# A Fourier mixer and a squared-ReLU feed-forward on one core: the end of the first batch under the order table, squares on GpSimd, two more tiles by seven products

## Chip, cores and metric

The kernel runs on one core of one Trainium2 chip. The metric is the device time of one execution in microseconds (us). Before the change it is 809.88 us, the median of three runs (809.78 to 810.07). The core has five engines that matter here: TensorE (PE, with its weight loads PEld), VectorE (DVE), ScalarE (ACT), GpSimd (POOL) and SyncE (SP, which issues DMAs). PE writes PSUM banks; ACT and DVE read them; GpSimd works on SBUF alone.

## What is computed

```python
X = np.fft.rfft(x, axis=1)                       # x: 8 batches x 3008 x 256
Yr = Xr @ w_r - Xi @ w_i + b_r
Yi = Xr @ w_i + Xi @ w_r + b_i                   # both soft-thresholded at 0.01
y = np.fft.irfft(Y, n=3008, axis=1)
...
h = y.reshape(24064, 256) @ w_in                 # 256 -> 2048
r = np.maximum(h, 0.0)
out = (s * (r * r) + b) @ w_out                  # 2048 -> 256, float32
```

## The kernel before

**The two transforms.** 3008 is taken as 94 x 32, so each transform is a DFT over 94, one over 32, and back, all as matrix products in float16. Batches 1 to 7 go through four stages (`s1_units`, `s23_units`, `s4_units`) whose results pass through DRAM (tiles u/us and v/vs); they are cut into small units and laid between the products of the feed-forward. Batch 0 has nothing to hide behind, so `first_batch` (L550) runs it by itself: twelve steps of `mix` (L602), `fwd_dft` (L630: products into a PSUM bank, a ReLU into m on ACT, a combination into z on DVE) and `inv_dft` (L656: products, then a copy into vt), then `turn` (L674: a transposition by a product with the identity, and a copy into vs) and `last_dft` (L690: products with C_t, and a copy into yt). yt holds y; the feed-forward reads it.

**The feed-forward** goes by 47 tiles of 512 rows (`_tile_order`, L139; tiles 0 to 3 are the "wide" ones of batch 0). For each tile `first_mm` (L1125) makes h in pairs of PSUM banks (psh): two 128x512 products for each of 16 blocks of 128 hidden columns. For each pair of blocks a ReLU takes the two banks to an SBUF tile rt (three of them in turn; L1154 on ACT or L1156 on DVE), and a square takes rt to gt (L1163 on ACT or L1165 on DVE). The second product of tile i is laid between the first products of tile i+1. It has two forms. `second_mms` (L1241) uses 64 products of 128x256. `seven_mms` (L1340) splits the 512 rows and the 256 output columns in halves and uses seven half-size products instead of eight, 112 products of 128x128; for that DVE makes eight sums and differences of parts of gt for each tile (`s_op`, L1306, L1325; the fourth kind may be a DMA with addition instead, issued from POOL, L1317), T_s holds the combined weights, and seven additions (L1390) take the results out, where the direct form needs two (L1278). `seven(ti)` (L1473) chooses: tiles 3 to 45 by seven, tiles 0, 1, 2 and 46 directly.

**What sets the order.** Up to the end of `first_batch` a framework schedules each engine's instructions, and the first of ACT and DVE to be free by a running cost sum takes a copy (`evac`, L233; `act_first`). Behind it `pe["on"]` is set (L1490) and the order is written out by hand: PE's order is the order of the Python code, and each other piece of work is recorded by `later` (L266) and emitted where the table `TURNS` says, which gives for each piece its delay in the sequence and its engine. `need` only asserts that a piece has been emitted. Waits come from data and from buffers: a PSUM bank is written again only when its readers are done.

**Banks.** While batch 0 runs, four single banks form the pool psm (`mix_bank`), two psf (`one_bank`), two psa (`other_bank`). When `first_batch` returns, psm is closed, and its space becomes two pairs of banks, psh (`two_banks`), for the first products.

**The end of batch 0.** All of `first_batch` but `rest` (the last turns and last_dfts) is ahead of the hand-written part. The units of stage 1 of batch 1 (`more`: one 94-row product of 512 columns and a copy into u each) are used there as filler by `some` (L717); the 9 slots from slot 0 on take the others.

Of the kernel before, what the change touches and what calls it, by code (L numbers as in the profile page):

```python
# [26 lines left out]
    "1t1t221o251l1p1y1k251o1s251h1q2i2q362q181p18181t151820181p1c203o1l201g1l294f7b1b3b1b3j15151h"  # L27
    "101p1x0w11150w201h0w14182w192h3h5m564v7j590l0p0x111m12221i000h042c7h0d0l0p0t1u121a1y040o1o08"
    "0p0d0t19213e262e2q050p0w2c0l1519212a2y3a2e080s280c0l2t3y4a090p0t1h2a2y2i1m081029090l0t1h2529"
    "3m4e2q2e0w1g002i040o191c3811191h1x3i2u1y420o0w181p4y260h0t0x1d1h1x262u361y04360s180p0x2p141s"  # L30
    "11151d1h3e2q2a2u0g111l0w1g111h1t292e3e2e2q0t360s182p363e0l0x19191h413p2x31080w1t0c0p151t2d2d"
    "352t35081e080q0c350k0w1k2k101y111a1c1k1l2k2d2i32141e2i2u3i4i0w160t0s1p153i101o0x1x141g1i151g"
    "1l1k1s1h3m4y191i1t2p111s1t10181v15203s141m1x0x102l1p191p2t14181c1m1d2q101c341f63191l1c1s1h3e"
    "175n1d1d1h181l212l3u0x1h1q2y0s0s1w0p260s450s1d0t0y161l210w2w0x1w2h0z0w2k1h0t0w1h3t1d0w1w1d1l"
    "1s1l1p201t1j5z1c1l1l1l1k1o1h1x1l321g1p1g2c1h1h1p212i36222i0s1s0p0u0s2d2l1g310p340x1517141s1x"
    "19101h1v1t1x252935423m4a320g1p0x0w101c101p15141k150z5r1l15181w1d21181l192y1k2k1h1h1p2d3e2i3q"
    "2q0s3q0o110p0y0k1l2d0w1k0t0w3t0z151s2d1p0x0w1v1l1c1s201g1x1l3q191l1t1x2h3m3a4m2e0s180w161828"
    "0x11141518201529151p196q1t1y19181s1c1h1s241h1q1h21212h19212l3d463y4m3a10240d0c4a0n0o0y0o2d11"
    "0l0o13150p0s1k0w0x101k2k191h1p2149354d3125312d250c2y0g100h0p0y0p102g1t3d0h1p4i2a1u0c0u0g2k0w"
    "1d2i1g25151e1m11212h0w1g2c1d1g1q3a3u3l2d2m0s2g190l1d11101l101114282e3y191i1420111h1l1x1l2p1g"  # L40
    "1p1y1c1g1h1u1k24191u2d2h1d1o3k1d1h1j1k1o2k1t1h1g1r1h1p1g2k1h1l1m1p1x2h1j5v1c1l1k201h3y1f5z1c"
    "1p1d1c1o1t251615192q1d141w151a181l15161t29182w191c291b182w1l1114211j1h101t1d1o291p1o241l1n6z"
    "1k1t1l1t1k1t1l2h1t1y1c1l181o1h1x25293m2q2y260w1g0t0y0w1x29102h14240p0x39102g1p0x101h1n1p1h1p"
    "29313q363q3y0c1k0x0w1019181x15141g150z6z1l19181o1p1x151l213a1g1k1d1l1x1x2a363e3m0w3q0w180l1y"
    "0s1l2d14380h0l150r11142s1l0x141r1h141h2s1c251d421h1h1p2d2h3y3i2u2e0o0x0w3m101s0x0l0w1h0w1k21"
    "2d0l3t0x2m1l260t0w1k141h1s241d1q1h1l2h2x1h1x293h463m464e10240h0g460r0s120s30190x0o17190t0w1l"
    "101114182k191h1p212x4d2h2x3p1t1t2d0g6e0k1s0h0s2i0h0s2g1l3p0l111u164e0o420s290p191i141w111a1i"
    "1m1u0p1p290k142o1d141i3a3a3h2d2i0k2c150d1d110k1t1d0x0w202q3u1x26142011191c25191l1w1h2y1c1s1g"
    "1q1p24151q2d2p181d381l1c1r1c1w2x1t19181v1l1c1l2g1g1p1i1o1o2h2j6f1d1h1g2o1d1e1f631g1l1c1g2k1d"
    "1p2215191i1h14211d1i1k1s191i1t1x1g3015292917182x19111o21130t0w1p191o2c1o21281h1j771c2d1h1l1o"  # L50
    "2k1d1h1t1y181l182c1h1l252d2m3m2m2u0w1k0t0y0p1p2h0t2l0w281d0p1n0w2k1t0x0w1p1r1p1p1x2l35424a3i"
    "320c1l0t1010180x311h101c110v5b191g0w1h112d181p1x22101g19293p414e4m5e4u0w1m0w180l0u0l191l142w"
    "0l0k0x0r0x0w30190p0w1f1p0s0w290x1d1g6q151d1t2d3h4u3y423e0w150w4u0w1c0s0t0w11141c0t1x0t290p2u"
    "113u0h0g100k11181k151q111x1x2l0x212x3d4i423e3q0g20050s460f0s3q0s2w0x0l0k0z150t0s1h0w0x10141s"
    "191h1x254l2x3l292p3d3p2p0h1q0o100l0o0y0p142c39410l0x221m4m0y1y4m081y08250h112i101w0x1a1i1m0s"
    "1t2d0s1c281d1c1m3q3u3125560s20150d1b11141h1l1118202a3y101a101w111d1h1o1h1t1h1p2q181l1c1m1c1o"
    "1h222d2p1d1g351l1d1r1c1k2w1t1d1g1z1l1c1g2s1k1p1i1p1o1w1n6b1h1l1x2k1h3i1f4z1c1h181c2819292m11"
    "151e140x201016181p191m1p251c301d2d2x1f101c1d0t1s2131150w1s191p281k1k241h1j771d1p1t1l1o2g1l1t"
    "1h321c1l1c2g1d1h1p2d2u323i2a0s190p0u0s1p2h0w2h0w1w1d0p1j0w381t0x1g1p1r1t1l1x2d353q3y4a320c0s"
    "0t10111d143d1h101c110v571910182g1519181l192q14281d1h4d4l4u5i525i0t120o110l1210191t142s0l0k0x"  # L60
    "0r0t0s2o150t0s170x0o0w2h0x1h142i0t191d252p3q463q4q0o1k0w4q0s1g150t111h141c2d2l0t290x1215260l"
    "0o140t1g1k1w1h221h1x252l1925313h3q4a3y4e142c0l0k1m0r0s120s34110p0w171h11101p1419181g201h1p1x"
    "252x3l3t2x311x3h1t0p4q0o100l0o3q0p0w2c1t3h0l0p320k0y0k250w191i181w0x1a11212p101k2w1l1k1y3a3u"
    "1j2c2m102g190l1d150w211g1115282e2i1c1m1824151h1l291p2p1k1l2u1g1k1l1u1k20191m292d1d1o301d1h4t"
    "1g1k291p1d1c1r1h181o2d1l1p1i1k1l1s2b5z181l1c1s1h46175f1d1p19181t1h212q101h1q0w101s101i141h11"
    "1i1p25182s1d1s2t1f102p1d0t1l1x2d150s1w191g1w1p24281p1j6z1h2l1h1t1k2g191p1d42181l182l1d1h1l1t"
    "263a2i220s180t160o252l102h102w150t1f0w2s1p15141l1n1t1h1p292h3a3q2i36081o11111024111d1p102s15"
    "17571d1w1c1x191d1g1p1x261k2l191l1x4l4q52565a0o1m0s1g0p0u0s1h1t141w0p0o3t0v0t0s1o190t0x1f110s"
    "181s0x2118720t111x2d2p2u4a3a2q0h1c0s4q0s1w0p0t0w0x0w1k2d310p2l0x1i0x1i0x0w1c0x1d1c1w1d1i1g1t"
    "212l191h3d3p3y424a4i1020110g0q170s3y0w1c150p0p171d0t18200s151d1024191h1p214l294125292x2l2l0c"  # L70
    "220w1w0h0s1a0h0s28313p0p1h4y1i4y0t5y0o2g0p111a0w1p1122321e1i1y0q0c1h250c102k19101e323e35292i"
    "0g250x09190t0c1s100t10281y2i1t221824151h1l211p2p1k1t2i1g1k1l1u1k21191y292h1c1k381h1g1n1k1o3d"
    "1t1h1g1v1l1c1l211g1l1m1o1o2c1l1o1s2g1h3a1h1p1h1k2g2h2t2215191e1c1128142a1g1x1d1i212d1k301h20"
    "2l1f1c2o1p151c251n1d141x1h1s201o1p241p1o211l1p1s251p391l1u1g1t1k1s1l1p1x2d3m2u322a101k0x1210"
    "1h29142l18241d111n14381t1h1o1x1x1h1t292h313i323y3m0k0w0x0x0w1c111l151424111t141c2t111p1d1x1p"
    "1u1c1s1l252d455m4q5246105y0w1g0t0y0w1d1h101s0p142d0r110s20110p13150p0s290w1p15151h2d314e3y36"
    "3e0g0w191i0s100p141h181o0x25141h1136191c1o1h1p1w1p1y1c1l212h1h212t354a3u363e0o100t13143m101k"
    "110t0w13151d141g191h1k1w1h1l1t213x2x253d3l251t1t0s1s0p0s2y0p0o1w152t193y1a3e1e0k240l191m1820"
    "151i1m1q212h1k0x2s151s1y3236290w281h0t1j190w1s1d1h2036361c1t1d1h1k241h1p1d1m181l1s241p1u2d2h"
    "1d1o381d1h1j1k1o2d1p1h1k1v1h1g1o2c1p1p1p1o1x1l1s1s291p1p1p1o1s1w1x2d1h1p2q1p1g211h39411c1o19"  # L80
    "1e1t211g20151f1c2g1l19291l1c1g1h1h211o2d1l1t1k1s1l1x1x2u1g1t1k1o1p1u1x251k28151n1o2d1t1h2p1l"
    "1k1w1h1k1p1o2l1l1p1o1w1l1l1p1u1s1s1t1w1p1y21251o28191n1o291t1h2p1l1k1x1l1k1o1o2c1l1p1o241l1l"
    "41421h1l1k1o1h1m1t1x1g2d151f1g1o1h192p1d1g1w1d1c1p1o1w1l1t1w291l1p1p2u2e1u1m1u141h1k1s1l1y21"
    "211o2k19391k1s1l1d2d1h1h1t1h1g1k1o281l1p1o1x1l1x3l3q1g1l1k1o1h1m1t1x1g24151f1g2d1h192d1d1g1w"
    "1h1k2c1o1s1l1p1p1t1x1y1k241o211l1m1t1u1x221l1q1t1u"
# [64 lines left out]
def kernel(  # L150
# [115 lines left out]
    def later(emit, cost, needs=(), frees=None):  # L266

        op = SimpleNamespace(emit=emit, cost=cost, needs=list(needs), gone=False)
        if frees is not None:
            reads[id(frees)].append(op)  # L270
        if pe["on"]:
            pieces.append(op)
            return op
        e = min(cost)
        if "act" in cost:
            e = "act" if act_first(cost["act"], cost["dve"]) else "dve"
            work(e, cost[e])
        begin(op, e)
        return op
# [270 lines left out]
    def first_batch():  # L550
# [49 lines left out]
        zt = {}  # L600

# [28 lines left out]
        def fwd_dft(ec, u):  # L630
            ps = one_bank().rearrange("p (j e) -> p j e", j=4)
            g = gs.pop((ec, u))
            for j in range(4):
# [12 lines left out]
            pos = mpool.tile([P, 4, P], F32, name="m", tag="m")  # L646
            nc.scalar.activation(out=pos, in_=ps, func=AF.Relu, bias=neg_lam)
            z = gpool.tile([P, 4, P], F16, name="z", tag="gt")
            nc.vector.scalar_tensor_tensor(
                out=z, in0=ps, scalar=LAM, in1=pos, op0=ALU.add, op1=ALU.min  # L650
            )
            work("act", 0.69)
            work("dve", 0.69)
            zt[(ec, u)] = z

        def inv_dft(ec, u):  # L656
            ps = other_bank()
            z = zt.pop((ec, u))
            for j in range(4):
                matmul(  # L660
# [925 lines left out]
```

## Time and profile before

| | us |
|---|---|
| median of three runs | 809.88 |
| the profiled execution, its own time | 810.04 |
| its span (first to last instruction) | 808.2 |
| PE busy in the span | 799.2 |
| DVE busy | 758.9 |
| ACT busy | 749.4 |
| POOL busy | 107.0 |
| first product of the feed-forward starts | 44.85 |
| last matrix product starts | 804.08 |

The profiled execution took 810.04 us, 1.84 us more than its span, and stands 0.16 us above the median. A timeline row gives start, duration, engine, line, what is written and read, and how many instructions were merged. A matrix product's duration has its latency in it (0.22 us for 128 columns); products follow each other faster than that, so what one costs PE is read from the start of one to the start of the next. Likewise ACT and DVE start the next instruction some 0.08 to 0.11 us before the row of the last one ends.

### The profile page before, as it was taken

To read this page: it belongs to the slowest core of one execution; us is meant where nothing else is said; L and a number is where in the kernel's file an instruction comes from. 1 tells how busy PE (TensorE), PEld (TensorE's weight loads), DVE (VectorE), ACT (ScalarE), POOL (GpSimd) and SP (SyncE) were. 2 spreads that over 40 slices of the span, in tenths; PEclk is the share of its full clock that TensorE was granted. 3 is DMA by queue.
4 is the path that set the end of the run, shared out by engine and by line. 5 is a ranking of instruction groups with operands and counts; after the bars stand their busy time and mean duration, and the time that the engine had idled before them with its cause. 6 is when DMAs were issued, how large, how long until landed. Compare 5 with 4: busy or idle time off the path is not lost.

```text
span 808.2 us, 22126 instructions
## 1 busy us (share of the span) xinstructions
PE 799.2 (99%) x9006; PEld 613.1 (76%) x9006; DVE 758.9 (94%) x1342; ACT 749.4 (93%) x932; POOL 107.0 (13%) x151
## 2 busy tenths in 40 slices
PE   8999999999999999999999999999999999999998
PEld 7857767777777977788777886778867788777876
DVE  5899999999999999999999999999999999999895
ACT  5989999999999999999999999999999999998984
POOL 4540001110110101111011210012000100000000
PEclk9999999999999999999999999999999999999999
DMA  8983387555774658665686666666556434732213
GB/s 205 190 194 78 95 237 184 102 136 153 208 151 86 153 139 226 145 124 113 169 200 145 135 145 161 152 154 136 137 164 177 108 80 119 183 67 58 62 41 79
DMA packets 120766, 112.89 MB, mean 140 GB/s; under 512 B 9933, under 2 KB 98129, under 8 KB 120665
## 3 DMA queue, kind: packets, MB, share of 16 engines
q1 hardware_dynamic: 102409, 80.55, 36.0%
q0 software_dynamic: 18256, 30.94, 23.2%
q8 instruction: 70, 1.15, 0.6%
q14 instruction: 31, 0.25, 0.1%
HBM read 53.52 MB, written 46.66 MB: 124 GB/s over the span
## 4 chain that ended last, share of the span: by engine, by line
PE 93%; DMA 0%; ACT 0%; DVE 0%; issue 0%; DVEq 0%; ACTq 0%
PE psh L225 40%; PE psa L225 34%; PE psf L225 19%; DMA out_dram<-ost 0%; DVE ost L1278 0%; ACT rt L1154 0%; ACT u L288 0%; DVEq L1278 0%; ACTq L1154 0%
## 5 line engine op out<-in xcount | busy, mean ns | idle before, releaser
L225 PE MATMUL psh<-yt,w_in 128*128 128x512 f16 (+3 forms) x1792 | 444.5, 343 | 0.2 <-ACT rt L1154 0.2
L225 PEld LDWEIGHTS <-gt 128*128 128x128 f16 x4400 | 306.7, 98 | 141.7 <-DVE gt L1325 2.4
L1154 ACT ACTIVATE rt<-psh 128x1024 f32<-128x1024 f32 x339 | 346.9, 1025 | 23.7 <-PE psh L225 21.5
L1163 ACT ACTIVATE gt<-rt 128x1024 f16<-128x1024 f32 x277 | 289.6, 1059 | 3.1 <-DVE rt L1156 0.7
L225 PE MATMUL psa<-w_out_t,gt 128*128 128x128 f16 (+1 forms) x2208 | 199.6, 224 | 0.0
L225 PEld LDWEIGHTS <-w_in 128*128 128x128 f16 x1824 | 152.0, 98 | 15.8 <-issue 1.4
L225 PE MATMUL psa<-T_s,gt 128*128 128x128 f16 x1824 | 144.3, 219 | 0.0
L1317 POOL DMA_DIRECT2D gt<-gt x63 | 54.8, 870 | 650.0 <-DVE s L1325 194.3
L1165 DVE TENSOR_TENSOR gt<-rt 128x1024 f16<-128x1024 f32 x99 | 120.0, 1216 | 2.4 <-ACT rt L1154 2.1
L1390 DVE SCALAR_TENSOR_TENSOR ost<-psa,s_bc,bias_bc 128x256 f32<-128x256 f32 x152 | 72.6, 478 | 6.7 <-PE psa L225 5.7
L1325 DVE TENSOR_TENSOR gt<-gt 128x1024 f16<-128x1024 f16 x109 | 74.4, 682 | 0.7
L1390 DVE SCALAR_TENSOR_TENSOR ost<-psa,s_bc,ost 128x256 f32<-128x256 f32 x129 | 61.6, 477 | 4.0 <-PE psa L225 3.8
L1325 DVE TENSOR_TENSOR gt<-gt,s 128x1024 f16<-128x1024 f16 x86 | 58.8, 684 | 1.4 <-PE psf L225 0.8
L1325 DVE TENSOR_TENSOR s<-gt 128x1024 f16<-128x1024 f16 x86 | 58.7, 683 | 0.5 <-ACT gt L1163 0.2
L880 DVE TENSOR_TENSOR ring<-psf,s 128x512 f16<-128x512 f32 x84 | 57.5, 685 | 1.7 <-PE psf L225 1.0
L225 PEld LDWEIGHTS <-s 128*128 128x128 f16 x688 | 45.4, 98 | 17.6
L225 PE MATMUL psa<-T_s,s 128*128 128x128 f16 x688 | 52.4, 219 | 0.0
L225 PE MATMUL psf<-W_g,xf 128*128 128x256 f16 x336 | 50.4, 273 | 0.0
L1156 DVE TENSOR_SCALAR rt<-psh 128x1024 f32<-128x1024 f32 x37 | 45.0, 1219 | 3.3 <-PE psh L225 1.6
L225 PEld LDWEIGHTS <-xf 128*128 128x128 f16 x504 | 44.7, 98 | 3.3
L225 PE MATMUL psf<-x,A_t 94*96 94x512 f16 x103 | 39.3, 382 | 0.3 <-DVE u L288 0.2
L225 PE MATMUL psf<-C_t,vs 96*128 96x96 f16 x484 | 38.3, 205 | 0.3 <-DVE u L288 0.3
(116 smaller groups left out, 836.6 us busy)
## 6 DMA issues: line engine op xcount, KB each, us to landing
out_dram<-ost SPq DMA_DIRECT2D x74, 256.0 KB
gt<-gt POOLq DMA_DIRECT2D x63, 256.0 KB, 4.0
ud<-u SPq DMA_DIRECT2D x56, 192.0 KB
us<-ud SPq DMA_DIRECT2D x28, 384.0 KB
vd<-v SPq DMA_DIRECT2D x42, 256.0 KB
vs<-vd SPq DMA_DIRECT2D x28, 384.0 KB
x<-in_x_dram POOLq DMA_DIRECT2D x56, 188.0 KB, 5.6
ring<-ring SPq DMA_DIRECT2D x120, 64.0 KB
```

Source lines behind the costliest of these rows:

```text
L225: return nc.tensor.matmul(out, lhs, rhs, **how)
L880: lambda e: nc.vector.tensor_tensor(out=ring[0][:, i % 4], in0=ps, in1=hold[i // 2][:, i % 2].unsqueeze(1).to_broadcast([P, 2, D]), op=ALU ...
L1154: nc.scalar.activation(out=rt, in_=ps, func=AF.Relu)
L1156: nc.vector.tensor_scalar(out=rt, in0=ps, scalar1=0.0, scalar2=None, op0=ALU.max)
L1163: nc.scalar.activation(out=gt, in_=rr, func=AF.Square)
L1165: nc.vector.tensor_tensor(out=gt, in0=rr, in1=rr, op=ALU.mult)
L1317: nc.gpsimd.dma_start(out=a12, in_=a11, accum_op=ALU.add)
L1325: nc.vector.tensor_tensor(out=out, in0=a, in1=b, op=op)
L1390: ins = nc.vector.scalar_tensor_tensor(out=out(), in0=hold[of], scalar=s_bc[0:size], in1=other(), op0=ALU.mult, op1=ALU.add,)
```

## The change

1. **End of batch 0.** `fwd_dft` and `inv_dft` record their work with `later`. The last steps of `first_batch` (the last forward and the last two inverse DFTs, half of the turns of the second column half, the other last_dfts) become a list `pre`, which runs behind the pool change and under the table, as far as the table's engine and order go. In it two new forms use pairs of banks: `turn_two` (eight transpositions and one copy of 1024 columns instead of two times four and 512) and `two_units` (`doubles`: two products of stage 1 and one copy of 1024 columns). The last copy into vt is split in two halves of 256 columns. The other units of stage 1 go to the first 8 slots instead of the first 9.
2. **Squares on GpSimd.** In tile 0 the squares 2, 4 and 6, and in tiles 1 to 3 the squares 1, 3 and 5 (of 0 to 7), are given to POOL as a product of rt with itself.
3. **Seven products** for tiles 1 and 2 too.
4. **The table** is another one throughout; it decides where ACT, DVE, SP and POOL do each piece in all tiles.

```diff
@@ later
-        if "act" in cost:
+        if len(cost) > 1:
             e = "act" if act_first(cost["act"], cost["dve"]) else "dve"
+        if e in load:
             work(e, cost[e])
@@ inv_dft
+            if (ec, u) == steps[-1]:
+                for h in range(2):
+                    r = slice(HW * h, HW * h + HW)
+                    vt_ops[h].append(leave_bank(
+                        vt[:, ec, r, 16 * u : 16 * u + 16], ps,
+                        ps.rearrange("p (k n) -> p n k", n=N2)[:, r], 256,
+                    ))
+                return
@@ first_batch
+        def turn_two(n):
+            ps = two_banks()
+            need(vt_ops[0])
+            for j in range(8):
+                matmul(
+                    ps[0:96, j // 4, j % 4 * P : j % 4 * P + P], vt[:, 1, n + j, :], eye_t,
+                    start=True, stop=True,
+                )
+            turned[(1, n)] = turned[(1, n + 4)] = leave_bank(
+                vs[(0, 0)][:, n : n + 8, P : 2 * P], ps,
+                ps[0:96].rearrange("p b (j e) -> p (b j) e", e=P), 1024,
+            )
...
+        pre = [
+            do(fwd_dft, *steps[-1]), doubles[0], do(inv_dft, *steps[-2]), do(last_dft, 0, 16),
+            doubles[1], do(inv_dft, *steps[-1]), do(last_dft, 0, 20), do(last_dft, 0, 24),
+            do(turn_two, 0), do(turn_two, 8), more[4], more[5], do(last_dft, 1, 0),
+            do(last_dft, 1, 4), do(last_dft, 1, 8), do(last_dft, 1, 12), more[6],
+            do(last_dft, 0, 28), more[7], doubles[4], more[10], more[11], more[12],
+        ]
@@ s1_units
+        def two_units(i):
+            c, j = divmod(4 * i, XCH)
+            bank = two_banks()
+            for k in range(2):
+                matmul(
+                    bank[0:96, k], A_t[0:N1, :],
+                    x16[(b, c)][0:N1, (j + 2 * k) * D : (j + 2 * k + 2) * D],
+                    start=True, stop=True,
+                )
+            u = upool.tile([P, UCH, D], F16, name="u", tag="u")
+            u_ops.append(leave_bank(
+                u[0:96], bank, bank[0:96].rearrange("p b (j d) -> p (b j) d", j=2), 1024,
...
@@ first_mm
+            elif e == "pool":
+                nc.gpsimd.tensor_tensor(out=gt, in0=rr, in1=rr, op=ALU.mult)
...
+        cost = {"act": 0.1 + 512 / 600.0, "dve": 0.065 + 512 / 480.0}
+        if mc // 2 in {0: (2, 4, 6,), 1: (1, 3, 5,), 2: (1, 3, 5,), 3: (1, 3, 5,)}.get(ti, ()):
+            cost = {"pool": 2.4}
@@ seven
-        return 3 <= ti < len(tiles) - 1
+        return 1 <= ti < len(tiles) - 1
@@ body
-    schedule(0, 9, more)
+    for u in pre:
+        u()
+    schedule(0, 8, more)
```

More of the change, by code (lines that the diff above doesn't have):

```diff
@@ L32 @@
[L32 to L36, printed above, removed]
@@ L600, in first_batch @@
         zt = {}
+        z_done = {}
+        vt_ops = [[], []]
         def mix(ec, u):
@@ L645, in fwd_dft, with above, below @@
                     )
[L646 to L654, printed above, removed]
+            def above(e):
+                zt["m"] = mpool.tile([P, 4, P], F32, name="m", tag="m")
+                nc.scalar.activation(out=zt["m"], in_=ps, func=AF.Relu, bias=neg_lam)
+            def below(e):
+                zt[(ec, u)] = gpool.tile([P, 4, P], F16, name="z", tag="gt")
+                nc.vector.scalar_tensor_tensor(
+                    out=zt[(ec, u)], in0=ps, scalar=LAM, in1=zt["m"], op0=ALU.add, op1=ALU.min
+                )
+            m_op = later(above, {"act": 0.69}, frees=bank)
+            z_done[(ec, u)] = later(below, {"dve": 0.69}, needs=[m_op], frees=bank)
         def inv_dft(ec, u):
             ps = other_bank()
+            need([z_done[(ec, u)]])
             z = zt.pop((ec, u))
@@ L674, in turn @@
         def turn(ec, n):
-            ps = mix_bank() if ec == 0 else any_bank() if n < HW else one_bank()
+            ps = mix_bank() if ec == 0 else one_bank()
+            need(vt_ops[n // HW] if ec else [])
             for j in range(4):
@@ L712, in last_dft @@
             y_ops[0].append((n, 4, done))
-        more, rows_1 = s1_units(1, True)
-        more.append(rows_1)
-        def some(n):
-            for _ in range(n):
-                if more:
-                    more.pop(0)()
         steps = [(ec, u) for ec in range(DC) for u in range(U)]
-        for i in range(2 * U + 2):
-            if i < 2 * U:
-                left = mix(*steps[i])
+        for i in range(2 * U):
+            left = mix(*steps[i])
             if i == 0:
@@ L747, in first_batch, with do @@
                     sum_w_out()
-        turn(1, 0)
-        turn(1, 4)
-        some(2)
-        turn(1, 8)
-        turn(1, 12)
-        some(2)
-        for n in range(0, HW, 4):
-            last_dft(1, n)
+        more, rows_1, doubles = s1_units(1, True)
+        more.append(rows_1)
+        def do(f, *args):
+            return lambda: f(*args)
+        pre = [
[5 more added lines that the diff above has]
+        ]
+        del more[:13]
         rest = [lambda n=n: turn(1, n) for n in range(HW, N2, 4)]
         rest += [lambda n=n: last_dft(1, n) for n in range(HW, N2, 4)]
-        return rest, more
+        return pre, rest, more
     def s1_units(b, more_banks=False):
@@ L1170, in first_mm @@
         )
+        cost = {"act": 0.1 + 512 / 600.0, "dve": 0.065 + 512 / 480.0}
+        if mc // 2 in {0: (2, 4, 6,), 1: (1, 3, 5,), 2: (1, 3, 5,), 3: (1, 3, 5,)}.get(ti, ()):
+            cost = {"pool": 2.4}
         squares.append(later(
-            square, {"act": 0.1 + 512 / 600.0, "dve": 0.065 + 512 / 480.0}, needs=[first]
+            square, cost, needs=[first]
         ))
@@ L1485 @@
         pools["m"] = pool
-        rest, more = first_batch()
+        pre, rest, more = first_batch()
     pools["h"] = ctx.enter_context(
```

156 lines of the change are left out of this document (85 added, 71 removed).

## The prediction

> **What bounds the kernel now.** First the page's busy times and its chain of work that ended last:
>
> ```profile
> PE 799.2 (99%) x9006; PEld 613.1 (76%) x9006; DVE 758.9 (94%) x1342; ACT 749.4 (93%) x932; POOL 107.0 (13%) x151
> ...
> PE 93%; DMA 0%; ACT 0%; DVE 0%; issue 0%; DVEq 0%; ACTq 0%
> ```
>
> The chain lies on PE nearly everywhere. A busy PE need not be PE at its peak, so next the timeline of PE in the steady part, read from start to start:
>
> ```profile
> 154.05 0.59 PE L225 MATMUL psh<-yt,w_in 128*128 128x512 f16 x2
> 154.48 0.61 PE L225 MATMUL psa<-T_s,gt 128*128 128x128 f16 x8
> 154.93 0.60 PE L225 MATMUL psf<-W_g,xf 128*128 128x256 f16 x4
> 155.37 0.59 PE L225 MATMUL psh<-yt,w_in 128*128 128x512 f16 x2
> ```
>
> Two products of 512 columns take 0.43 us, eight of 128 take 0.45, four of 256 take 0.44. Over all rows the usual spacings are 0.2158, 0.0558 and 0.1092 us (0.0825 for 192 columns, 0.042 for 96). These times the program's 9006 products give 790.67 us; what start-to-start time is more than that I call waiting. It is 12.4 us: 7.2 in the first 37.3 us, 3.25 from there to 60 us, 1.94 in the 744 us behind. So PE is the bound by its own work, and only its work or its waits ahead of 60 us can give much. Then the table by stretches of time (PE, PEld, DVE, ACT, POOL busy us):
>
> ```profile
> 40.00:50.00 10.00, 8.69 (x63) 4.69 (x62) 9.87 (x16) 7.73 (x14) 7.64 (x9) 1.00 0.94 208
> 50.00:60.00 10.00, 9.97 (x84) 6.71 (x84) 10.00 (x12) 9.40 (x12) 1.29 (x4) 1.00 0.68 189
> 70.00:80.00 10.00, 10.00 (x85) 7.49 (x83) 9.28 (x23) 9.40 (x13) 0.00 (x0) 1.00 0.26 67
> 500.00:600.00 100.00, 100.00 (x1170) 77.56 (x1168) 97.68 (x175) 95.53 (x119) 11.32 (x16) 1.00 0.63 147
> ```
>
> DVE and ACT have little to spare, yet at 97.7% DVE still holds PE up for only 0.2 us in 100.
>
> **Seven products for tiles 1 and 2.** Each loses 64 products of 256 columns (64 x 0.1092 = 6.99 us) and gets 112 of 128 (112 x 0.0558 = 6.25). That is 0.74 us a tile, **1.48 us** for two. No other product is added or lost: the changed program's 9102 come to 789.19. What it costs is on DVE, and what the squares cost on POOL has to come from sums there; the groups by line and shape (after the bar: busy us, mean ns):
>
> ```profile
> L1165 DVE TENSOR_TENSOR gt<-rt 128x1024 f16<-128x1024 f32 x99 | 120.0, 1216 | 2.4 <-ACT rt L1154 2.1
> ...
> L1325 DVE TENSOR_TENSOR s<-gt 128x1024 f16<-128x1024 f16 x86 | 58.7, 683 | 0.5 <-ACT gt L1163 0.2
> ...
> L521 POOL TENSOR_TENSOR acc<-acc,w_out_t 128x512 f32<-128x512 f32 x5 | 5.8, 1165 | 0.3 <-DMA w_out_t<-in_moe_w_out_dram 0.2
> ```
>
> A sum of 0.683 us takes 0.60 from start to start. The program has 18 more on DVE (8 a tile, and 2 that were DMAs from POOL), 10.8 us, and 14 evictions of 256 columns (0.395) for 4 of 512 (0.658), 2.9 us.
>
> **Squares on POOL.** Twelve leave ACT and DVE: ACT has 13 fewer (0.947 apart, 12.3 us) and DVE one more (1.13). Relus and copies are handed round by the table. Over the whole kernel, by such spacings, ACT loses 1.5 us and DVE gains 1.0. I summed each engine's work in program order up to what needs the first 60 us of PE work from 37.3 us on: DVE goes from 57.7 to 59.4 us, ACT from 54.7 to 53.1. DVE starts that work at 39.3, PE ends it at about 100.2, so DVE is left with 1.5 us of idle time in 61, 2.4%, as much as the row of 500 to 600 leaves it with PE unharmed. So I cost the sums at nothing: PE's own work hides them, and any DVE delay beyond those 1.5 us goes to PE.
>
> No row shows POOL squaring 1024 columns. Twice the 1.107 us spacing of L521's 512-column sums is 2.2, twice that of the sums into W_g (1.25) is 2.5; I take 2.2 as the nearest form. The three rt tiles go round, so a POOL square holds the relu three pairs later. I followed tile 0 with these times: the third relu ends at 49.8 and its square on POOL at 52.1; the relu that writes the same rt next needs products that end at 52.1 as well, so it loses nothing. At the next POOL square DVE's relu waits 0.25 us, PE does not. In POOL's queue two loads of batch 2's x stand behind three squares, the other six behind four or more; they go out up to 15 us later, and are used from about 100 us on. SP's writes of u come 1.1 us earlier, with the last u copy.
>
> **End of batch 0.** PE's order is the same up to 37.31 us. Before, it waits there for copies, several times (timeline):
>
> ```profile
> 37.31 0.34 PE L225 MATMUL psm<-C_t,vs 96*128 96x96 f16 x4
> ...
> 37.72 0.68 DVE L288 CAST vs<-psm 96x512 f16<-96x512 f32 x1
> ...
> 37.86 0.40 PE L225 MATMUL psa<-T_t,z 128*128 128x128 f16 x4 [0.21 <-DVE z L649]
> ...
> 41.17 0.42 PE L225 MATMUL psa<-small,vt 128*96 128x128 f16 x4 [0.22 <-DVE vt L239]
> ...
> 43.57 0.33 PE L225 MATMUL psa<-C_t,vs 96*128 96x96 f16 x4 [0.27 <-DVE vs L288]
> 44.17 0.33 PE L225 MATMUL psf<-C_t,vs 96*128 96x96 f16 x4 [0.27 <-DVE u L288]
> ```
>
> After it, the next product goes to a pair of banks, and the pool of pairs opens only when the last reader of psm is done: the vs copy at 37.72, over at 38.40. Nothing else can pass in PE's queue, so PE stands from 37.31 to about 38.46, **1.15 us of a new wait**. I then walked the program with row durations (0.06 us from a copy's end to PE, ACT 1.02 and DVE 1.21 us for a copy of 1024 columns, by their relus of that size, L1154 and L1156). Next: the two vt copies let the first turn_two go at 40.60 (waits of 0.09 and 0.22); DVE's 1024-column copy of its result ends at 42.49, and the first last_dft behind it waits 0.58; later ones 0.26 and 0.12; the first relus, seven in a row on ACT, hold PE 0.16, 0.23 and some hundredths. Together 2.9 us, for 3.25 before: **0.3 us** gained. The waits move rather than go; the first product of the feed-forward starts at 45.55 with more of the stage-1 work done.
>
> **The sum.** 810.04 - 1.48 - 0.3, with the waits behind 60 us as before, is 808.2 for an execution like the profiled one. That one stood 0.16 above the median, so **808.1 us**, 0.22% less. The first 37.3 us and the last 4.1 (the last evictions and stores) stay. By the errors of the walk (0.5) and waits that the new table adds or takes (up to 1 us) its own range is 807.0 to 809.6.
>
> **Rivals.**
>
> *POOL squares shut DVE out.* Mechanism: a POOL square reads SBUF twice, and so do DVE's squares, sums, ring steps and T_s: 31.5 of the 59.4 us above. If the two cannot read at once, each POOL square keeps DVE's next two-input instruction waiting. DVE passes about one other instruction (0.6 us) and then waits 1.6 of the 2.2: 12 x 1.6 = 19 us at most, and half of that if the squares fall on PSUM copies. It decides from 1.5 us of lost DVE time on, in tiles 0 to 3; PE would come 8 to 17 us late. Price: **820 us** (815 to 825), slower. What the trace has on it is one overlap:
>
> ```profile
> 46.68 1.16 POOL L521 TENSOR_TENSOR small<-acc,w_out_t 128x512 f16<-128x512 f32 x1
> ```
>
> ```profile
> 47.73 1.21 DVE L1165 TENSOR_TENSOR gt<-rt 128x1024 f16<-128x1024 f32 x1
> ```
>
> The DVE square starts 0.11 us before the POOL sum's end and takes its usual 1.21. That is against it, but short, and ends on POOL are rough; elsewhere DVE reads PSUM while POOL sums. So blocking may cost from nothing to 19 us, and I take nothing, by this row. The Trainium skill (SBUF — State Buffer, Who interferes with whom) has this as a rule: a DVE instruction with two SBUF inputs and a GpSimd instruction that reads SBUF exclude each other for a whole instruction, and whichever came first holds the port. By that rule the kernel gets slower, to about 820; the trace of before neither shows nor excludes it.
>
> *POOL is just late.* With 2.5 us a square and DVE's 1.5 us used up, the relus that wait for rt hold PE 0.1 to 0.3 us at each of twelve squares: 1.2 to 3.6 us, so 809.3 to 811.7, say 810.5.
>
> *The table does more.* If the new order also takes most of the 1.94 us of waits behind 60 us, 806.6. Against: at most 0.6 of them are single waits that I can find, the rest is 0.2 us in 100, near the spacings' rounding.
>
> That the change does not do what it says is excluded for the products and squares, which are counted in the program. For the end of batch 0 it is half my forecast already.
>
> **Chances.** Forecast 0.60, late POOL 0.14, shut-out 0.19, table 0.07. 0.2% (1.62 us, about what a measurement of this kernel can tell from no change) puts the border of faster at 808.26. Of the forecast 0.34 lies below it and 0.26 above; the table's 0.07 is below; late POOL gives 0.10 same and 0.04 slower (above 811.5); the shut-out is slower. Faster 0.41, same 0.36, slower 0.23. The range, 806.2 to 816, takes in all but the upper part of the shut-out.
>
> **What would show it.** Right: 9102 products; PE standing about 1.1 us at 37.3; the first psh product of yt at about 45.5; POOL squares of 2.2 to 2.5 us, and DVE rows beside them as long and as dense as elsewhere; no waits of PE over 0.1 us from 56 to 120 us. Wrong: DVE sums or squares that start only when a POOL square ends, or are longer than 0.69 and 1.22 us beside one; PE waiting for DVE or POOL between 50 and 110 us; a sum of waits from 37.3 to 60 us far from 2.9.

## The result and the profile after

The changed kernel takes **818.05 us**, the median of four runs (817.67 to 820.17), beside 809.98 us (809.78 to 811.08) for the kernel before on the same chip: a ratio of 1.0101, 95% interval 1.0088 to 1.0113. It is 1% slower, 10 us above the forecast of 808.1 and 2 us above the range. The profiled execution has a span of 815.8 us.

The page of the changed kernel: busy times, and the chain of work that ended last.

```profile
PE 800.8 (98%) x9102; PEld 612.5 (75%) x9102; DVE 769.5 (94%) x1352; ACT 748.5 (92%) x934; POOL 132.2 (16%) x161
...
PE 87%; DVE 7%; DMA 2%; POOL 1%; issue 1%; ACT 0%; SPq 0%; DVEq 0%; ACTq 0%; POOLq 0%
```

PE has the 9102 products of the forecast, and by the spacings of the prediction they come to 789.19 us, 1.48 less than before. But the chain has left PE for 13% of the span, where it was 7%. DVE's busy time is 10.6 us up, and PE waits 21.4 us where it waited 12.4. The table of stretches tells where (PE, PEld, DVE, ACT, POOL busy us). Before:

```profile
60.00:121.00 61.00, 61.00 (x510) 44.17 (x508) 57.81 (x112) 56.44 (x76) 2.95 (x5) 1.00 0.51 136
```

After:

```profile
60.00:121.00 61.00, 55.78 (x518) 38.80 (x517) 60.39 (x115) 48.97 (x66) 23.77 (x19) 1.00 0.51 118
```

PE lost 5.2 busy us here and its waits, counted from start to start, are 9.2 us where they were 0.1. (The first expectations below say 10.6 for this stretch; counted up to 121 us it is 9.2.) DVE, 95% busy before, is busy for 99% of it; ACT has 12 us to spare. Elsewhere nothing is new: waits of 6.9 us ahead of 36.5 us, 3.3 from there to 60 us (before 3.2), 2.0 behind 121 us.

Then the groups of DVE between 60 and 121 us, by line and shape (after the bar: busy us, mean ns). The first ring step (L899 before, L948 after), the sum of two spectra xf (L840, L889) and a part of T_s (L514, L516), before:

```profile
L899 DVE TENSOR_TENSOR ring<-ring,low 128x512 f16<-128x512 f16 x12 | 5.0, 420 | 0.2
...
L840 DVE TENSOR_TENSOR xf<-xf 128x256 f16<-128x256 f16 x12 | 3.3, 284 | 0.4 <-ACT xf L288 0.4
...
L514 DVE TENSOR_TENSOR T_s<-w_out_t 128x1024 f16<-128x1024 f16 x2 | 1.4, 682 | 0.0
```

After:

```profile
L929 DVE TENSOR_TENSOR ring<-psf,s 128x512 f16<-128x512 f32 x12 | 8.2, 683 | 0.0
L948 DVE TENSOR_TENSOR ring<-ring,low 128x512 f16<-128x512 f16 x12 | 7.2, 601 | 0.2
...
L889 DVE TENSOR_TENSOR xf<-xf 128x256 f16<-128x256 f16 x12 | 4.4, 375 | 0.0
...
L516 DVE TENSOR_TENSOR T_s<-w_out_t 128x1024 f16<-128x1024 f16 x2 | 2.9, 1434 | 0.0
```

The same instructions take 30 to 110% longer on average, but only those that read SBUF twice; L929, which reads PSUM and SBUF, keeps its 0.68. The timeline of the changed kernel beside one POOL square shows the step:

```profile
65.70 0.68 DVE L929 TENSOR_TENSOR ring<-psf,s 128x512 f16<-128x512 f32 x1
...
65.87 1.89 POOL L1214 TENSOR_TENSOR gt<-rt 128x1024 f16<-128x1024 f32 x1 [1.65 <-ACT rt L1203]
...
66.42 1.63 DVE L948 TENSOR_TENSOR ring<-ring,low 128x512 f16<-128x512 f16 x1
...
67.97 0.28 DVE L889 TENSOR_TENSOR xf<-xf 128x256 f16<-128x256 f16 x1
...
68.30 0.11 PEld L226 LDWEIGHTS <-xf 128*128 128x128 f16 x2 [0.42 <-DVE xf L889]
```

POOL begins its square at 65.87. DVE's instruction on PSUM runs beside it at full speed. Its next one, the ring step with both inputs in SBUF, begins at 66.42 and takes 1.63 us instead of 0.42: it ends 0.29 us after the POOL square. The xf sum behind it is late, and PE waits for that sum. Eleven of the twelve squares have such a DVE row beside them, longer by 0.4 to 1.5 us (squares 1 and 2 share one). What DVE rows are longer than their group's median comes to **9.2 us**, 0.77 a square (the two rows of the T_s group are one long and one of usual length, so that one counts half; with the whole of it the sum is 10.0). No other DVE row is more than 0.1 us longer. Take the usual length off a long row's end, and the moment that is left lies 0.13 to 0.14 us before the POOL row's end, in each of them: there DVE is let go (as far as the ends of POOL rows can be trusted).

It goes the other way round, too. Where DVE keeps two-input instructions coming, the POOL square is the one that waits (3.14 us instead of 1.89; three such DVE rows beside it, from 83.47 to 84.83, keep their usual length):

```profile
83.45 3.14 POOL L1214 TENSOR_TENSOR gt<-rt 128x1024 f16<-128x1024 f32 x1 [0.74 <-ACT rt L1203]
```

### The profile page after: what moved, and what is told of

Same layout as the page of the kernel before. It is cut to its first block, busy times and chain, and to the rows that moved or that the text cites. A ratio compares the mean times of both kernels' runs of the same rounds, so it can differ in the third digit from the quotient of the medians.

```text
span 815.8 us, 22352 instructions
## 1 busy us (share of the span) xinstructions
PE 800.8 (98%) x9102; PEld 612.5 (75%) x9102; DVE 769.5 (94%) x1352; ACT 748.5 (92%) x934; POOL 132.2 (16%) x161
## 4 chain that ended last, share of the span: by engine, by line
PE 87%; DVE 7%; DMA 2%; POOL 1%; issue 1%; ACT 0%; SPq 0%; DVEq 0%; ACTq 0%; POOLq 0%
PE psh L226 37%; PE psa L226 31%; PE psf L226 18%; DMA x<-in_x_dram 1%; PE psm L226 1%; DVE gt L1379 1%; POOL gt L1214 1%; DVE ost L1444 1%; DVE ring L948 0%; POOL x L369 0%; DVE ring L929 0%; DVE gt L1216 0%; DVE ring L952 0%; DMA ring<-ring 0%; DVE u L290 0%
## 5 line engine op out<-in xcount | busy, mean ns | idle before, releaser
L1203 ACT ACTIVATE rt<-psh 128x1024 f32<-128x1024 f32 x344 | 352.3, 1026 | 24.6 <-PE psh L226 20.9
L1212 ACT ACTIVATE gt<-rt 128x1024 f16<-128x1024 f32 x264 | 276.3, 1061 | 2.4 <-DVE rt L1205 0.4
L226 PE MATMUL psa<-w_out_t,gt 128*128 128x128 f16 (+1 forms) x2176 | 187.9, 221 | 0.5 <-DVE ost L1444 0.4
L226 PE MATMUL psa<-T_s,gt 128*128 128x128 f16 x1920 | 152.3, 219 | 0.7 <-DVE gt L1379 0.6
L1379 DVE TENSOR_TENSOR gt<-gt 128x1024 f16<-128x1024 f16 x119 | 82.5, 694 | 1.0 <-PE psh L226 0.5
L1444 DVE SCALAR_TENSOR_TENSOR ost<-psa,s_bc,bias_bc 128x256 f32<-128x256 f32 x160 | 76.6, 479 | 7.2 <-PE psa L226 5.8
L1444 DVE SCALAR_TENSOR_TENSOR ost<-psa,s_bc,ost 128x256 f32<-128x256 f32 x135 | 64.5, 478 | 5.5 <-PE psa L226 5.1
L1379 DVE TENSOR_TENSOR gt<-gt,s 128x1024 f16<-128x1024 f16 x90 | 61.7, 685 | 1.1 <-PE psf L226 0.2
L1379 DVE TENSOR_TENSOR s<-gt 128x1024 f16<-128x1024 f16 x90 | 61.5, 684 | 0.5 <-ACT gt L1212 0.3
L929 DVE TENSOR_TENSOR ring<-psf,s 128x512 f16<-128x512 f32 x84 | 57.5, 684 | 0.4 <-PE psf L226 0.2
L1205 DVE TENSOR_SCALAR rt<-psh 128x1024 f32<-128x1024 f32 x32 | 39.0, 1219 | 1.3 <-POOL gt L1214 0.6
```

The source lines that it names most:

```text
L226: return nc.tensor.matmul(out, lhs, rhs, **how)
L929: lambda e: nc.vector.tensor_tensor(out=ring[0][:, i % 4], in0=ps, in1=hold[i // 2][:, i % 2].unsqueeze(1).to_broadcast([P, 2, D]), op=ALU ...
L1203: nc.scalar.activation(out=rt, in_=ps, func=AF.Relu)
L1205: nc.vector.tensor_scalar(out=rt, in0=ps, scalar1=0.0, scalar2=None, op0=ALU.max)
L1212: nc.scalar.activation(out=gt, in_=rr, func=AF.Square)
L1379: nc.vector.tensor_tensor(out=out, in0=a, in1=b, op=op)
```

## Experiments

In all of them "longer DVE rows" is what rows exceed their group's median by, and waits of PE are start-to-start times above the spacings. Theory A is the shut-out, B the load of the 18 more sums and of the new order. The first four stand beside the same runs of the kernel before (median 810.47 us).

**1. The squares done by ACT.** Edit, in `square`: `if e == "act"` becomes `if e in ("act", "pool")`.

> The changed kernel with its twelve POOL squares done by ACT at the same places of the order; nothing else differs. Theory A (a POOL square shuts DVE's two-SBUF-input instructions out; in the changed kernel 9.2 us of DVE rows longer than their group's median lie beside the twelve squares): every DVE row has its usual length again (no ring step over 0.70 us), and PE's waits from 60 to 121 us, 10.6 us in the changed kernel, fall. They do not go to nothing: ACT takes 12 x 0.95 = 11.4 us more, on 53.1 us of work in a stretch of 61, 3.5 us too much. 811 to 813.5 us. Theory B (the 18 more sums and the new shares of the table overload DVE, POOL's squares cost nothing): DVE's work is unchanged, so the 10.6 us of waits stay and the ACT work comes on top: 818 to 822 us.

Measured 815.68 us, ratio 1.0065 (1.0048 to 1.0082): between the two ranges, in neither. No DVE row is longer. Waits from 60 to 121 us fall from 9.2 to 5.3 us. The profile puts 2.2 us of them down to an engine, and 2.0 of these are ACT's (1.1 us for its copy of v, 0.5 for yt, 0.4 for s). A's direction, and less of the gain than A expected: ACT, now busy for 59.3 of the 61 us, can't take 11.4 us without delay either.

**2. The squares done by DVE.** Edit: the branch for POOL goes, so that POOL's places fall to DVE.

> The changed kernel with its twelve POOL squares done by DVE at the same places of the order. Theory A: DVE loses 12 x 1.13 = 13.6 us to the squares in place of the 9.2 us that it lost beside them, so PE is 4 to 5 us later than in the changed kernel: 821 to 824 us, that is, the squares on POOL had cost DVE two thirds of what doing them itself costs. Theory B: DVE has no time left and gets 13.6 us more: 829 to 833 us.

Measured 822.25 us, ratio 1.0142 (1.0126 to 1.0158), as A expected and 7 us under B. The step of 4.2 us from the changed kernel is about what 13.6 us of squares cost beyond the 9.2 us that POOL's squares took from DVE. But it does not lie where that sum has it: waits from 60 to 121 us are 9.3 us, about as in the changed kernel, and 2.3 of the 3.4 us of added waits lie between 36.5 and 60 us.

**3 and 4. POOL reads, and POOL fills, added to the kernel before.** No other engine's work changes. Edit, at the end of `square`, for the same twelve pairs (the first line in both, then the lines of 3 or of 4):

```diff
+                nc.gpsimd.tensor_copy(out=spare[0:1, 0:1], in_=gt[0:1, 0, 0, 0:1])
+                some = w_in_t[0][:, 0:768]
+                nc.gpsimd.tensor_tensor(out=spare, in0=some, in1=some, op=ALU.mult)   # 3
+                for _ in range(2):
+                    nc.gpsimd.memset(spare, 1.0)                                      # 4
```

> The kernel before, with one product of 768 columns of w_in_t with themselves (two f16 inputs) on POOL added behind each of the twelve squares 2, 4, 6 of tile 0 and 1, 3, 5 of tiles 1 to 3; a copy of one element of gt ahead of it places it in time, its result is not used. No work of another engine changes. Theory A: each takes about 1.4 us, three quarters of a POOL square, and costs DVE some 0.77 x 0.75 = 0.6 us, 7 us in all, of which DVE's idle time of 3.3 us in the stretch can hide a part: 812.5 to 817 us, with ring steps, xf sums or squares longer than usual beside the POOL rows. Theory B: no difference, 809.5 to 810.5 us, and DVE rows of the usual length.

> The same additions to the kernel before, but each POOL product is replaced by two fills of 768 columns (f16), which read nothing; together about as long, 1.46 us by the fill of 1024 columns at the start (0.97 us). Theory A, with reading as its cause: no difference, 809.5 to 810.5 us, DVE rows of their usual length. If any POOL work at all shuts DVE out: as with the products, 812.5 to 817 us. Theory B: no difference.

With reads, whose result nobody uses: 814.37 us, ratio 1.0044 (1.0028 to 1.0060), 5.6 us of longer DVE rows, waits from 60 to 121 us 3.4 us (before 0.1). Its profiled execution has 1.5 us more waits ahead of 36.5 us, too, on the first loads of x, where no read was added. With fills: 809.84 us, ratio 0.9988 (0.9978 to 0.9997), waits 0.1 us. The timelines, first of the kernel with reads, POOL and then DVE:

```profile
70.01 1.52 POOL L1170 TENSOR_TENSOR spare<-w_in 128x768 f16<-128x768 f16 x1
```

```profile
69.78 0.43 DVE L899 TENSOR_TENSOR ring<-ring,low 128x512 f16<-128x512 f16 x1
70.25 1.57 DVE L903 TENSOR_TENSOR ring<-ring,high 128x512 f16<-128x512 f16 x1
71.85 0.43 DVE L907 TENSOR_TENSOR ring<-ring 128x512 f16<-128x512 f16 x1
```

and of the kernel with fills:

```profile
72.26 1.53 POOL L1170 MEMSET spare<- 128x768 f16 x2
```

```profile
72.75 0.42 DVE L907 TENSOR_TENSOR ring<-ring 128x512 f16<-128x512 f16 x1
73.08 0.42 DVE L899 TENSOR_TENSOR ring<-ring,low 128x512 f16<-128x512 f16 x1
73.53 0.42 DVE L903 TENSOR_TENSOR ring<-ring,high 128x512 f16<-128x512 f16 x1
```

The same ring steps, beside 1.5 us of POOL each: 1.57 us in place of 0.43 beside a read, 0.42 beside fills. Reading is the cause, and it needs neither the sums nor the new table.

**5. The reads alone taken out of the changed kernel.** POOL stays in its places for at least as long; the twelve squares are left out. Edit:

```diff
-                nc.gpsimd.tensor_tensor(out=gt, in0=rr, in1=rr, op=ALU.mult)
+                one = gt[0:1, 0, 0, 0:1]
+                nc.gpsimd.tensor_copy(out=one, in_=rr[0:1, 0, 0, 0:1])
+                nc.gpsimd.memset(gt, 1.0)
+                nc.gpsimd.memset(gt, 1.0)
+                nc.gpsimd.tensor_copy(out=one, in_=rr[0:1, 0, 0, 0:1])
```

> The changed kernel with each of the twelve POOL squares replaced, at the same place and behind the same wait, by a copy of one element from rt, two fills of the whole gt block (which read nothing; by the fill at the start of the kernel 0.97 us each) and another copy of one element from rt, which holds rt to the end. Those twelve squares are not computed. POOL is busy at the same places for about 2.3 us, so it is late at least as long as in the changed kernel, and the 18 more sums, the table and the end of batch 0 are unchanged; only the long reads of SBUF by POOL are gone. Theory A (the reads shut DVE out, and the order leaves no room for it): no lengthened DVE row, waits of PE from 60 to 121 us under 1.5 us instead of 9 to 10, and the time that was forecast: 808 to 809.5 us. Rivals (POOL late, the load of the sums, the order of the table): 815 to 819 us.

Measured 810.95 us, ratio 1.0010 (1.0001 to 1.0019). The kernel is 0.5 us above the kernel before on its chip, where the changed kernel was 8.1 above. The loss is nearly gone with the reads, though POOL is busier than in the changed kernel and the sums, the table and DVE's load are the same:

```profile
60.00:121.00 61.00, 60.58 (x606) 44.29 (x602) 59.64 (x126) 54.77 (x75) 31.38 (x46) 1.00 0.63 151
```

DVE is 98% busy and PE waits 1.7 us in this stretch. That rules B out as the main cause. A's range is missed by 1.45 us all the same, and its 1.5 us of waits by 0.2; 36.5 to 60 us has 3.9 us of waits, 0.78 of it one relu that waits for rt. Since twelve squares are left out, this shows what the reads cost and is no kernel to use.

**6. The same with one fill.**

> As squares_filled, but with one fill and without the second copy from rt, so that POOL's part takes 1.2 to 2 us where the two fills and two copies of squares_filled took 2.4 to 4.7 us and the square itself 1.9 to 3.1. The twelve squares are not computed. It asks where the 2.3 us come from that squares_filled has more waits than forecast. If from POOL's part being longer than a square (rt held in tile 0, where a relu waits for it and PE 0.78 us, and later starts): PE's waits between 36.5 and 121 us fall from 5.6 to 3 to 4 us and the time to 808.2 to 809.6 us. If from the 18 more sums and the order of the table: unchanged, 810.5 to 811.5 us.

Measured 810.51 us (809.66 to 813.58), ratio 1.0007 (0.9999 to 1.0016). Waits from 36.5 to 60 us 3.1, from 60 to 121 us 1.0: 4.1 us, just over the expected 3 to 4. The time missed its range by 0.9 us, and just reaches the other one (810.5 to 811.5), so it tells less than the waits; the profiled execution (811.07) has 0.5 us more waits ahead of 36.5 us than the changed kernel, 0.9 more behind 121 us and 0.5 more after the last product.

**7. Smaller POOL instructions.** Edit: the square in four products of 256 columns.

> The changed kernel with each POOL square in four instructions of 256 columns. Theory A, with an exclusion that lasts for one POOL instruction: a quarter is some 0.5 us, so a DVE row is lengthened by at most that, and DVE comes in between; the DVE time lost falls from 9.2 us to 3 to 6, and the time to 812 to 816 us, with some POOL quarters lengthened instead. If the exclusion lasted for the whole series: as the changed kernel, 817 to 819 us.

Measured 817.22 us, ratio 1.0087 (1.0074 to 1.0101). By the time alone that is the range of an exclusion that lasts for the whole series (817 to 819); the rows show that it lasts for one instruction only. In the timeline of DVE, beside a series of four from 95.28 to 98.15, three of the five two-input instructions (the last row holds two) are held up by 0.3 to 0.4 us each:

```profile
95.44 0.73 DVE L948 TENSOR_TENSOR ring<-ring,low 128x512 f16<-128x512 f16 x1
96.21 0.72 DVE L952 TENSOR_TENSOR ring<-ring,high 128x512 f16<-128x512 f16 x1
96.85 0.47 DVE L1447 SCALAR_TENSOR_TENSOR ost<-psa,s_bc,bias_bc 128x256 f32<-128x256 f32 x1
97.24 0.43 DVE L956 TENSOR_TENSOR ring<-ring 128x512 f16<-128x512 f16 x1
97.60 0.90 DVE L889 TENSOR_TENSOR xf<-xf 128x256 f16<-128x256 f16 x2
```

DVE's loss only falls to 7.4 us (3 to 6 were expected), since more instructions are hit, and the series is longer (2.87 us for 1.89), so POOL is late itself: one relu waits for rt in tile 0 and PE with it for 1.8 us.

**8. POOL reads with one input**, added to the kernel before. Edit: in place of the product of experiment 3, two `tensor_scalar` of 768 columns.

> The kernel before with additions on POOL at the same twelve places as in idle_reads, but with instructions that read one input, two scalings of 768 columns of w_in_t (f16) each; the row of 512 columns with f16 on both sides took 1.5 us, those from f32 0.61, so the two together take 1.8 to 4.5 us. If any long POOL read shuts DVE's two-input instructions out: lengthened DVE rows as in idle_reads, 813 to 818 us. If only POOL instructions with two inputs do: DVE rows of their usual length, 809.5 to 810.8 us.

Measured 813.82 us, ratio 1.0046 (1.0032 to 1.0060), 6.6 us of longer DVE rows. One input is enough. But these POOL rows are slow (2.13 us each), and DVE is let go in the middle of them (POOL, then DVE):

```profile
66.63 2.13 POOL L1170 TENSOR_SCALAR spare<-w_in 128x768 f16<-128x768 f16 x1
```

```profile
66.78 0.95 DVE L899 TENSOR_TENSOR ring<-ring,low 128x512 f16<-128x512 f16 x1
67.77 0.42 DVE L903 TENSOR_TENSOR ring<-ring,high 128x512 f16<-128x512 f16 x1
68.23 0.43 DVE L907 TENSOR_TENSOR ring<-ring 128x512 f16<-128x512 f16 x1
```

**9. Where DVE has time to spare.** 1 and 2 suggested that DVE or ACT are simply full. So tiles 1 and 2 were made direct again, with POOL's squares and without. Edit: `return 3 <= ti < len(tiles) - 1`, and the table moved over piece by piece, the two additions of each direct tile beside their neighbours.

> The same, but with the twelve squares on POOL as in the changed kernel. Theory A: DVE has 59.4 - 13.7 = 45.7 us of work in the stretch and loses some 9 us to the POOL squares, 55 of 61; PE does not see it: 809 to 811 us, with DVE rows lengthened beside the squares as before. Rival (POOL is late by itself: its squares of 1.9 to 3.1 us come too late for the products and hold rt too long, whatever DVE has to do): waits of PE ahead of products that read gt, and of relus for rt, as many as in the changed kernel: 815 to 819 us.

> The changed kernel with tiles 1 and 2 directly again (their 16 sums and 14 additions go, four additions of the direct form come, at the places that the table has for their neighbours) and the twelve squares on DVE at POOL's places: the new end of batch 0 and the new order alone, 9006 products. Theory A (shut-out, and behind it the load: with its squares back the changed kernel asks DVE and ACT for 124 to 125 us of work in a stretch of 61, which has 122): DVE has 59.4 + 13.6 - 13.7 = 59.3 us of work in the stretch, ACT 53.1, both fit, so the waits from 60 to 121 us vanish (under 1 us): 809.7 us by the 0.3 us gained before 60 us, 809.0 to 810.6. Rival D (the 5.3 us of waits that squares_on_act left there belong to the new order of the table, not to load): they stay here, 812 to 815 us.

Measured 816.77 us with POOL's squares, ratio 1.0080 (1.0067 to 1.0094), and 818.31 us with the squares on DVE, ratio 1.0102 (1.0087 to 1.0116). Both expectations by A fell. The first lies in the range of a POOL that is late by itself (815 to 819), but not by its signs: DVE is busy for 51 of the 61 us, PE still waits 6.1 us there, and the waits that the profile names are for copies and sums of DVE and, 0.8 us, for a load of vs, none for gt or for a relu. The second lies in no range. No DVE row of it is longer, DVE has 8.7 us to spare in the stretch, and PE waits 5.4 us there and 5.6 between 36.5 and 60 us (3.3 in the changed kernel). Their tables were moved by hand, so they don't tell what the changed kernel's own order costs. The cleanest test came last, in the unchanged order:

**10. The sums of tiles 1 and 2 left out.** Edit, in `s_op`: `if ti in (1, 2): return`; the products that used the sums read parts of gt, so the results of tiles 1 and 2 are left out.

> The changed kernel, squares on POOL, without the 16 sums of tiles 1 and 2 (their products read parts of gt in place of the sums, so the outputs of tiles 1 and 2 are not computed). DVE gets 16 x 0.6 = 9.6 us back in the stretch from 60 to 121 us, as much as the 9.2 us that its rows lose beside the POOL squares. If what counts is the sum of DVE's time (load): waits there under 2 us, 808.5 to 811 us. If what counts is the place, because a DVE instruction that is late by 1 us is waited for at once in this order: rows as long as before beside the squares, waits of 4 to 7 us there, 812.5 to 815.5 us.

Measured 815.78 us, ratio 1.0064 (1.0051 to 1.0078). The waits of 6.1 us are those of "place" (4 to 7), the time is 0.3 us above its range, and "load" (under 2 us of waits, 811 us at most) is missed by both. DVE's rows lose 9.4 us beside the squares, DVE has 5.4 us idle in the stretch, and still PE waits for single late pieces (waits of PE between 60 and 121 us):

```profile
PE psf L226 <- DVE ring L929: 0.9, 2, 0.7
PE psf L226 <- DVE xf L290: 0.9, 1, 0.9
PE psf L226 <- DVE xf L889: 0.6, 1, 0.6
```

**11. Neither long reads nor the sums.** Experiments 6 and 10 together.

> squares_filled_once without the 16 sums of tiles 1 and 2 (their outputs and the twelve squares are not computed): the forecast's PE work with neither long POOL reads nor more sums. If the 1 us of waits that is left from 60 to 121 us belongs to the sums: under 0.3 us there, about 3 us between 36.5 and 60, and 808.0 to 809.8 us; what then stands over 808.1 is scatter of the waits ahead of 36.5 us and of the end. If it belongs to the order of the table: unchanged, 810 to 811 us.

Measured 811.21 us (809.17 to 811.85), ratio 1.0004 (0.9995 to 1.0013): just above both ranges. Not under 0.3 us but 2.6 us of waits from 60 to 121 us, and most of it is something else again:

```profile
PE psf L226 <- DMA vs<-vd: 1.7, 1, 1.7
```

PE comes to the last transform of batch 1 before its rows are back from DRAM. PE is hardly early: it is ready at about 113.6 us and begins at 115.27; in experiment 6 it begins at 113.84 without a wait. So the rows come at least 1.4 us later here. The wait stands in other kernels too: 1.9 us in seven_from_3, 0.8 in seven_from_3_pool. What makes the load late was not settled. Without it 0.9 us of waits are left, for 1.0 in experiment 6: leaving out the sums gave nothing back that can be seen.

**12 and 13. Two attempts at a faster kernel.** seven_from_2 makes tile 1 direct and tile 2 by seven products, with no square on POOL; dma_sums keeps both tiles by seven, gives the squares to ACT and DVE, and some sums to DMAs that POOL issues. Edit of the second, in `s_op`:

```diff
-            if n == 4 and e == "pool":
+            if n == 4 and (e == "pool" or ti in (1, 2, 3)):
```

> The changed kernel with tile 1 directly and tile 2 by seven products, no square on POOL: of the twelve, six by ACT and six by DVE in turn. Theory A: DVE has 59.4 - 6.9 + 6.8 = 59.3 us of work in the stretch, ACT 53.1 + 5.7 = 58.8, both under 61; PE does 0.74 us less than in the kernel before: 809.0 us (808.3 to 811; the upper part since two engines are near full at once). Rival D (the table's order costs the waits): 812 to 815 us.

> The changed kernel with no square on POOL (of the twelve, eight by ACT and four by DVE) and with the fourth sum of each half of gt in tiles 1 to 3 as a DMA with addition issued from POOL, up to six DVE sums fewer. Theory A: POOL's DMA issues read no SBUF operands and lengthened no DVE row so far. ACT has 53.1 + 7.6 = 60.7 us in the stretch, DVE 59.4 + 4.5 - 3.6 = 60.3 of 61: just full, so PE is late by 1 to 4 us on the 808.2 us that its work gives: 809 to 812 us. If DMA issues from POOL shut DVE out too: 814 us and more.

Measured 815.81 us, ratio 1.0063 (1.0051 to 1.0076), and 817.76 us, ratio 1.0083 (1.0071 to 1.0096). In both no DVE row but one (0.1 us) is longer, so the second is not slow because POOL's DMA issues shut DVE out, though its time lies in that range. Both have 6.0 to 6.1 us of waits from 60 to 121 us, one piece of ACT or DVE at a time; the second has 2.4 us more than the changed kernel behind 121 us, 1.2 of it a wait for a DMA of the ring. My sums of load, which said that all fits into 61 us, predicted neither. No version of the change tried here is faster than the kernel before.

## Why the prediction was wrong

**The step that failed** is the cost of POOL's squares beside DVE. The prediction had the rival's mechanism, and from one overlap of 0.11 us at the end of a POOL row it wrote "blocking may cost from nothing to 19 us, and I take nothing, by this row". It costs 9.2 us of DVE time, and PE waits 9.1 us more between 60 and 121 us. Experiments 3, 4 and 5 show the cause by itself: reads added to the kernel before slow it, fills of the same length don't, and the reads taken out of the changed kernel take its loss from 8.1 us to 0.5. The Trainium skill (SBUF — State Buffer, Who interferes with whom) states this rule, for two SBUF inputs of DVE against any GpSimd instruction that reads SBUF but not against one that only writes; the traces agree on each count (1.63 us for 0.42 beside a read, 0.42 beside a fill, 0.68 for a DVE row with one input in PSUM), but not on its word that it lasts for the whole instruction: by the rows DVE is let go 0.13 to 0.14 us before a POOL square ends, and 1.44 us before the end of the slow rows of experiment 8.

So the overlap that was held against the rule could not test it: it lay in the last 0.11 us of a POOL row. In experiment 4 the same two instructions, which the edit doesn't touch, overlap by 0.60 us, and the DVE square takes 0.47 us longer (POOL, then DVE):

```profile
46.70 1.15 POOL L521 TENSOR_TENSOR small<-acc,w_out_t 128x512 f16<-128x512 f32 x1
```

```profile
47.25 1.68 DVE L1166 TENSOR_TENSOR gt<-rt 128x1024 f16<-128x1024 f32 x1
```

In seven_from_2 they overlap by 0.27 us, and the DVE square takes 1.35.

**The rival's price** was 820 us (815 to 825), by 12 x 1.6 us at most and half of that where squares fall on PSUM readers. 0.77 us a square is that half, and the measured 818.05 lies in its range. It had 0.19 of the chances, but the range stopped at 816, short of that price.

**"Any DVE delay beyond those 1.5 us goes to PE"** was too kind as well: DVE's spare time is no pool from which a delay is paid in full. In no_sums DVE's rows lose 9.4 us, it still has 5.4 us idle from 60 to 121 us, and PE waits 6.1 us. The pieces are ordered so that each ends shortly before PE needs it, with two psf banks in turn; PE waits at once for single late pieces, as experiment 10 lists them, and the idle time behind them gives back a part at most. "So I cost the sums at nothing" holds within 1 us: with the sums, without long reads and with twelve squares left out (experiment 6) DVE is idle for 1.4 us in 61, and PE waits 1.0 us.

**"POOL is just late"** cost nothing that the profile of the changed kernel shows. A POOL square takes 1.89 us when nothing stops it, less than the 2.2 assumed, and 2.18 on average with its own waits for DVE. (The 1.107 us behind the 2.2 is the step from a sum to a DMA issue; two sums in a row start 1.23 us apart.) In tile 0 a relu of DVE waits 0.59 us for a POOL square (0.25 in the walk) and one of ACT 0.42; PE waits for neither.

**Seven products** came out as counted: 9102 products, with the same spacings in the profile of after as before, so 789.19 us.

**The end of batch 0** came out as walked. The timeline of the changed kernel on PE:

```profile
36.87 0.22 PE L226 MATMUL psf<-g,F 128*128 128x128 f16 x1
38.06 0.63 PE L226 MATMUL psh<-x,A_t 94*96 94x512 f16 x2 [0.97 <-DVE vs L290]
```

The new wait is 1.14 us (forecast 1.15), and the next are 0.11, 0.23, 0.60, 0.24, 0.13, 0.16 and 0.30 (0.09, 0.22, 0.58, 0.26, 0.12, 0.16, 0.23 and some hundredths). All of it started 0.44 us earlier, with earlier loads of x. The 0.3 us of gain wasn't there: waits from 36.5 to 60 us are 3.3 us, 3.1 in experiment 6, and 3.2 before.

**What stays open.** With the reads gone, 810.5 to 811 us were measured and 808.1 forecast. The forecast was a gain of 1.8 us; beside the kernel before on the same chips (810.17 and 810.43) these are losses of 0.3 and 0.5, so 2.1 to 2.3 us are missing. In experiment 6, 1.2 us are waits between 36.5 and 121 us that the forecast didn't have. The rest was seen in profiled executions as a wait for vs, more waits ahead of 36.5 us and a later end, each differing from run to run. How much of it a median holds was not settled. Nor was it settled why the versions that give the squares to ACT or DVE, and lengthen no DVE row, keep 5 to 9 us of waits from 60 to 121 us: whether work that is full, or the order, or both.

## What to carry to other kernels

An instruction given to an idle engine is free only if that engine shares nothing with a busy one. Before moving elementwise work to GpSimd, count which DVE instructions beside it have both inputs in SBUF, and price each GpSimd instruction that reads SBUF at its length less what DVE can do from PSUM meanwhile (here 0.8 us for one of 1.9). In an order written so that each piece is just in time, much of a local delay reaches the end even where the engine has idle time (6.1 of 9.4 us in experiment 10), so a mean load says little. One short overlap in a trace is no evidence against a known rule; ask first whether it is long enough to show the effect.

## What the runs showed of the hardware that was not expected

- GpSimd with a single SBUF input holds DVE up as well (experiment 8), but in a slow instruction only for its first part: DVE's row ended 1.0 us before that POOL row of 2.13 us did. All 14 DVE rows that are held up there are let go 1.44 to 1.45 us before the POOL row's end, those beside a POOL square 0.13 to 0.14.
- The exclusion works in both directions: POOL squares took 1.89 to 3.14 us, the long ones where DVE kept two-input instructions coming.
- A fill, harmless to instructions with two inputs, does hold up a DVE copy. In the kernel of experiment 5 the f16 copies of 64x256 in the ring (0.22 us each) took 0.61 and, two in one row, 1.21 us beside fills of 0.95 us:

```profile
101.15 0.61 DVE L973 COPY ring<-ring 64x256 f16<-64x256 f16 x1
101.29 0.47 DVE L956 TENSOR_TENSOR ring<-ring 128x512 f16<-128x512 f16 x1
101.81 1.21 DVE L973 COPY ring<-ring 64x256 f16<-64x256 f16 x2
```

  The Trainium skill (SBUF — State Buffer, Who interferes with whom) has copies among the instructions that may run in a mode that takes both of DVE's port pairs, and then contend with any GpSimd instruction; these rows fit that.
